# Decode attention with a KV cache: the last batch's K tile goes back behind the V tile of four batches earlier in the load queue

## The chip, the cores and the metric

The kernel runs on one core of a Trainium2 chip. The metric is the device time of one execution in microseconds (us); the kernel before took 373.58 us, the median of 8 runs from 372.36 to 374.9 us.

## What is computed

Thirty-two batches, four query positions each, 32 query heads sharing four K/V heads, 2048 cached positions, head size 128, all in bf16. One batch's K cache and its V cache are 2 MB each.

```python
q = (x @ wq).reshape(B, Sq, Hq, Dh).transpose(0, 2, 1, 3)
k = jnp.repeat(k_cache, rep, axis=1)
v = jnp.repeat(v_cache, rep, axis=1)
scores = jnp.einsum("bhqd,bhkd->bhqk", q, k) * (Dh ** -0.5)
p = softmax(scores, axis=-1)
o = jnp.einsum("bhqk,bhkd->bhqd", p, v)
out = o.transpose(0, 2, 1, 3).reshape(B, Sq, Hq * Dh) @ wo
# B, Sq, D = 32, 4, 1024; Hq, Hkv, Sk, Dh = 32, 4, 2048, 128
```

## The kernel before

The kernel writes an operation list for each engine in program order; every operation names those it must wait for, and the helper class `_Program` turns names into semaphore waits. Each engine works through its own list in order. So does SP, the engine that issues nearly all the transfers[...].

**Loads.** The buffer `big` has eight slots of 2 MB. The query weights `wq` take slots 0 to 3 at the start. After that the list `loads` (lines 159 to 164) gives the order of the 64 K and V tiles: K of batches 0 to 2, then alternately the K tile three batches ahead (`LEAD`) and the V tile of the current batch. Two further lines, 163 and 164, take K of the last batch, 31, out and put it directly behind K of batch 30. The tail of the list is therefore K30, K31, V27, V28, V29, V30, V31, where K31 means the K tile of batch 31. Tile number n goes to slot (4 + n) mod 8 (line 168). Its issue waits until the tile that held the slot is used up: for a K tile, its last transpose, `("kt", b, 3)`; for a V tile, the last matmul of its product with the probabilities, `("pv", b)`. K31 has place 58, slot 6, and waits for `pv` of batch 23; V27 has place 59, slot 7, and waits for `kt` of batch 27.

**Output weights.** Behind the 64 tiles SP issues `wo` in ten chunks (line 185), of 4, 4, 4, 4, 4, 4, 4, 2, 1 and 1 heads. Eight heads fill one slot, and the slots follow on: chunks 0 and 1 go where V26 was, chunks 2 and 3 where K30 was, chunks 4 and 5 to slot 6, chunks 6 to 9 to slot 7. Each chunk waits for the tile that last held its slot. So chunks 4 and 5 wait for the transposes of K31, chunks 6 to 9 for `pv` of V27.

**One batch i.** The steps, each a function in the kernel:
- `qd(i)`: GpSimd puts the queries of the batch in block-diagonal form (line 262).
- `kt(i)`: VectorE transposes the K tile in four pieces (line 271).
- `pe_qk(i)`: TensorE computes the scores into `ps_s`, 16 matmuls (lines 283 and 16). It waits for all four pieces and for exp of the batch before, which frees `ps_s`.
- `softmax_max(i)` on VectorE (lines 291 and 292), `softmax_exp(i)` on ScalarE (line 296).
- `pt(i)`: VectorE transposes the probabilities (line 304).
- `pd(i)`: GpSimd (for the last batch mostly VectorE) spreads them into `PD_sb` (line 316), once `pv` of the batch before has read it.
- `pe_pv(i)`: TensorE multiplies them by the V tile in 64 matmuls (line 323).
- `o_evac`, `pe_ot`, `ot_evac`: scaling, transposing and storing the result for the projection (lines 330, 336, 340).

**Order in the loop.** The engines overlap batches. Iteration i puts, in this order: `qd(i+1)` on GpSimd; pieces 0 and 1 of `kt(i+1)` on VectorE; the scores of i on TensorE; the maximum on VectorE; exp on ScalarE; pieces 2 and 3 of `kt(i+1)` and `pt(i)` on VectorE; then `pe_pv(i-2)` on TensorE and `pd(i-1)` on GpSimd. Thus on TensorE the product with V of batch 27 stands in iteration 29, directly ahead of the scores of batch 30; and on VectorE the first two pieces of K31 stand in iteration 30, directly ahead of the maximum of batch 30.

**The end.** After the last iteration come `pe_pv` of batches 30 and 31, and then the output projection `oproj` (lines 351 and 16): two matmuls a head, all 32 heads, chunk by chunk. It needs the finished output of the last batch and chunk c of `wo`. The result is copied out of `ps_s` in two halves (lines 359 and 360) and stored.

Of the kernel before, what the change touches and what calls it, by code (L numbers as in the profile page):

```python
# [78 lines left out]
def bass_standalone__gqa_block_cached__sampling_kernel(  # L79
# [8 lines left out]
    B, Sq, D = x.shape  # L88
# [21 lines left out]
    with ExitStack() as es:  # L110
# [48 lines left out]
        loads = [("k", b) for b in range(LEAD)]  # L159
        for b in range(B):  # L160
            loads += [("k", b + LEAD)] if b + LEAD < B else []
            loads += [("v", b)]
        loads.remove(("k", B - 1))
        loads.insert(loads.index(("k", B - 2)) + 1, ("k", B - 1))
        slot_of = {}
        holder = {s: "w" for s in range(NW)}
        for n, (kind, b) in enumerate(loads):
# [292 lines left out]
```

## Time and profile before

| | |
|---|---|
| median of 8 runs | 373.58 us (372.36 to 374.9) |
| profiled execution, its own time | 373.94 us |
| its span, first to last instruction | 372.2 us |
| TensorE matmuls busy | 279.5 us (75%) |
| VectorE busy | 275.3 us (74%) |
| GpSimd busy | 164.6 us (44%) |
| ScalarE busy | 123.0 us (33%) |
| bytes moved | 151.90 MB, mean 408 GB/s |
| mean granted TensorE clock | 0.953 |

The span begins with the first instruction of the profiled execution and ends with its last; the rest of the execution's time, 1.74 us, lies around it. All moments in the text below are us from the start of the span. Busy shares are means over the whole span; the steps near its end are read from the timeline, which gives for each instruction its start, its length, its engine and line, and in brackets the idle time of the engine before it with what ended it.

### The profile page before, as it was taken

What the parts mean: (1) busy time and instruction counts of PE and PEld (TensorE: products, weight loads), DVE (VectorE), ACT (ScalarE), POOL (GpSimd) and SP (SyncE); (2) the same over time, 40 slices, a digit from 0 to 9 for tenths busy, and PEclk for the clock granted to TensorE, in tenths of its full rate; (3) what the DMA queues carried; (4) which work ended last, traced back from release to release, by engine and by line L of the source; (5) the groups of instructions that cost most, each with busy time, mean ns of one, the idle gap of its engine ahead of it and who ended that gap; (6) DMA issues with size and microseconds to landing.
All of it is one profiled execution on the core that took longest, in us unless ns stands there. A gap on an engine that the chain in (4) does not pass through costs nothing.

```text
span 372.2 us, 5961 instructions
## 1 busy us (share of the span) xinstructions
PE 279.5 (75%) x2744; PEld 144.3 (39%) x2272; DVE 275.3 (74%) x273; ACT 123.0 (33%) x135; POOL 164.6 (44%) x262
## 2 busy tenths in 40 slices
PE   1972557888777778888888787887777876589796
PEld 1001003444444444444444545444333533545622
DVE  0029677999999999999999878799888699554300
ACT  1010211444444443333333333433433144247200
POOL 5001050555555555555554363655555555067100
PEclk9997888999999999999999898999998999699989
DMA  8999999999999999999999999999999999999960
GB/s 329 428 430 437 426 424 424 431 430 425 422 428 431 424 424 428 425 428 430 424 426 430 427 424 429 421 431 430 424 426 424 430 430 424 428 428 386 387 242 28
DMA packets 14507, 151.90 MB, mean 408 GB/s; under 512 B 1297, under 2 KB 1553, under 8 KB 5777
## 3 DMA queue, kind: packets, MB, share of 16 engines
q1 hardware_dynamic: 14336, 151.39, 96.7%
q8 instruction: 20, 0.33, 0.4%
q10 hardware_dynamic: 144, 0.13, 0.1%
q14 instruction: 7, 0.05, 0.0%
HBM read 151.26 MB, written 0.26 MB: 407 GB/s over the span
## 4 chain that ended last, share of the span: by engine, by line
DMA 33%; PE 32%; DVE 19%; ACT 8%; issue 7%; SPq 1%
DMA big<-in_v_cache_dram 27%; PE ps_s L16 18%; DVE mx L291 13%; ACT P_sb L296 7%; PE ps_s L283 6%; DMA big<-in_wq_dram 6%; PE ps_r L323 5%; DVE KT_sb L271 3%; PE ps_s L351 2%; DVE negmx L292 1%; DVE PD_sb L316 1%; DVE QT_sb L244 1%; DVE KT_sb L228 1%; SPq L156 0%; ACT QT_sb L340 0%
## 5 line engine op out<-in xcount | busy, mean ns | idle before, releaser
L316 POOL COPY PD_sb<-PT_sb 32x1024 f32<-32x1024 f32 x121 | 125.8, 1040 | 138.6 <-DVE KT_sb L271 62.4
L271 DVE STREAM_TRANSPOSE KT_sb<-big 128x1024 f32<-128x1024 f32 x128 | 150.7, 1217 | 5.2 <-DMA big<-in_k_cache_dram 5.1
L323 PE MATMUL ps_r<-big,PD_sb 128*128 128x128 bf16 x1984 | 121.7, 224 | 32.6 <-DMA big<-in_v_cache_dram 29.8
L323 PEld LDWEIGHTS ps_r<-big,PD_sb 128*128 128x128 bf16 x1984 | 117.4, 101 | 40.0 <-POOL QD_sb L262 23.2
L296 ACT ACTIVATE P_sb<-ps_s,negmx 128x2048 bf16<-128x2048 f32 x32 | 81.6, 2550 | 81.8 <-DVE negmx L292 81.8
L16 PE MATMUL ps_s<-KT_sb,QD_sb 128*128 128x512 bf16 x384 | 107.4, 388 | 0.0
L291 DVE TENSOR_REDUCE mx<-ps_s 128x1 f32<-128x2048 f32 x32 | 73.3, 2292 | 25.8 <-PE ps_s L16 25.4
L283 PE MATMUL ps_s<-KT_sb,QD_sb 128*128 128x512 bf16 x128 | 49.8, 389 | 43.0 <-ACT P_sb L296 36.8
L283 PEld LDWEIGHTS ps_s<-KT_sb,QD_sb 128*128 128x128 bf16 x128 | 12.6, 99 | 121.1 <-issue 73.1
L340 ACT ACTIVATE QT_sb<-ps_r 128x128 bf16<-128x128 bf16 x32 | 23.5, 735 | 104.5 <-PE ps_r L336 104.5
L304 DVE STREAM_TRANSPOSE PT_sb<-P_sb 128x1024 f32<-128x1024 f32 x32 | 39.9, 1246 | 14.6 <-ACT P_sb L296 14.6
L262 POOL COPY QD_sb<-QT_sb 32x64 f32<-32x64 f32 x128 | 29.6, 231 | 41.7 <-DVE QT_sb L244 26.1
L330 ACT ACTIVATE o_sb<-ps_r,rinv 128x128 bf16<-128x128 f32 x32 | 11.9, 373 | 19.7 <-PE ps_r L323 19.7
L228 DVE CAST KT_sb<-ps_r 128x512 bf16<-128x512 f32 x2 | 1.3, 686 | 20.7 <-PE ps_r L212 20.7
L359 DVE CAST y_sb<-ps_s 128x512 bf16<-128x512 f32 x1 | 0.7, 692 | 21.4 <-PE ps_s L351 21.4
L351 PE MATMUL ps_s<-big,QT_sb 128*128 128x512 bf16 x32 | 13.2, 412 | 0.9 <-ACT QT_sb L340 0.9
L16 PE MATMUL ps_s<-big,QT_sb 128*128 128x512 bf16 x32 | 13.1, 411 | 0.0
L336 PEld LDWEIGHTS ps_r<-ident,o_sb 128*128 128x128 bf16 x32 | 3.1, 96 | 23.8 <-issue 21.6
L351 PEld LDWEIGHTS ps_s<-big,QT_sb 128*128 128x128 bf16 x32 | 4.7, 147 | 11.4 <-issue 11.2
L16 PE MATMUL ps_s<-big,P_sb 128*128 128x512 bf16 x32 | 9.1, 410 | 0.0
L230 ACT ACTIVATE KT_sb<-ps_r 128x512 bf16<-128x512 f32 x2 | 1.1, 595 | 24.2 <-PE ps_r L16 24.2
L212 PEld LDWEIGHTS ps_r<-big,P_sb 128*128 128x128 bf16 x8 | 0.8, 104 | 20.4 <-issue 12.3
(30 smaller groups left out, 68.4 us busy)
## 6 DMA issues: line engine op xcount, KB each, us to landing
big<-in_k_cache_dram SPq DMA_DIRECT2D x32, 2048.0 KB, 28.7
big<-in_v_cache_dram SPq DMA_DIRECT2D x32, 2048.0 KB, 31.8
big<-in_wq_dram SPq DMA_DIRECT2D x4, 2048.0 KB, 14.6
big<-in_wo_dram SPq DMA_DIRECT2D x7, 1024.0 KB, 19.6
big<-in_wo_dram SPq DMA_DIRECT2D x1, 512.0 KB, 12.6
big<-in_wo_dram SPq DMA_DIRECT2D x2, 256.0 KB, 10.2
P_sb<-in_x_dram SPq DMA_DIRECT2D x1, 256.0 KB, 2.6
out_dram<-y_sb SPq DMA_DIRECT2D x1, 128.0 KB, 1.8
```

What stands on the lines that cost most here:

```text
L16: return eng.add_instruction(mybir.InstMatmult(name=nc.get_next_instruction_name(), engine=eng.engine, start_tensor_calc=start, stop_tenso ...
L262: p.op("pool", lambda e, s=src, d=dst: e.tensor_copy(d, s), waits if g == 0 else [], ("qd", i) if g == G - 1 else None)
L271: p.op("dve", lambda e, s=src, d=dst: e.transpose(d, s), waits, ("kt", i, c))
L283: mm = lambda e, a_=(out_, lhsT, rhs), f=first, l=last: e.matmul(a_[0], lhsT=a_[1], rhs=a_[2], start=f, stop=l, skip_group_check=True)
L291: p.op("dve", lambda e: e.tensor_reduce(mx[:, i % 4:i % 4 + 1], ps_s[:, :], AX.X, ALU.max), [("qk", i)], ("mx", i))
L296: p.op("act", lambda e: e.activation(P_sb[:, :, :, :].rearrange("p t r w -> p t w r"), ps_s[:, :].rearrange("p (t w r) -> p t w r", w=2, r=R),
L304: p.op("dve", lambda e: e.transpose(dst, src), [("exp", i)] + ([("pd", i - 2, G - 1)] if i > 1 else []), ("pt", i))
L316: p.op("dve" if i == B - 1 and g < 3 else "pool", lambda e, s=src, d=dst: e.tensor_copy(d, s), waits, ("pd", i, g))
L323: p.op("pe", lambda e, t=t: e.matmul(buf[:, 0:Dh], lhsT=pd_of(i)[:, t // 2, :, :, t % 2].rearrange("p g q -> p (g q)"), rhs=big[:, slot_of ...
L330: p.op("act", lambda e: e.activation(o_sb[:, :], buf[:, 0:Dh], ACT.Copy, scale=rinv[:, i % 4:i % 4 + 1]), [("pv", i), ("rinv", i)] + ([("o ...
L340: p.op("act", lambda e: e.activation(oT_sb[:, i * Sq:(i + 1) * Sq, :].rearrange("p s h -> p h s"), buf[:, 0:128].rearrange("p (h s) -> p h ...
L351: mm = lambda e, a=(out_, lhsT, rhs), h=h: e.matmul(a[0], lhsT=a[1], rhs=a[2], start=(h == 0), stop=(h == Hq - 1), skip_group_check=True)
```

## The change

Two lines are deleted, and nothing else. K31 stays where the loop puts it: the tail of the list becomes K30, V27, K31, V28, V29, V30, V31. V27 now has place 58 and slot 6, K31 place 59 and slot 7. The waits of the two places and of all later tiles are as they were, since they come from the tiles that held the slots before. With the two contents exchanged, `wo` chunks 4 and 5 wait for `pv` of V27, and chunks 6 to 9 for the transposes of K31. In the changed kernel every line after line 162 has a number lower by two.

```diff
         for b in range(B):
             loads += [("k", b + LEAD)] if b + LEAD < B else []
             loads += [("v", b)]
-        loads.remove(("k", B - 1))
-        loads.insert(loads.index(("k", B - 2)) + 1, ("k", B - 1))
         slot_of = {}
         holder = {s: "w" for s in range(NW)}
```

## The prediction

> **What bounds the kernel now.** First the page's chain of work that ended last, to see which resources lie on the path:
>
> ```profile
> ## 4 chain that ended last, share of the span: by engine, by line
> DMA 33%; PE 32%; DVE 19%; ACT 8%; issue 7%; SPq 1%
> ```
>
> DMA leads, so I looked where the chain runs through a load for the last time. The chain in order of time over the tail (start, length, what) shows it:
>
> ```profile
> 288.59 31.86 DMA big<-in_v_cache_dram
> 320.45 0.14 issue
> 320.58 5.14 PE ps_r L323 x64
> ...
> 329.22 2.30 DVE mx L291
> ...
> 334.50 0.38 PE ps_s L283
> ...
> 347.49 3.75 PE ps_r L323 x64
> ...
> 353.35 0.41 PE ps_s L351
> ```
>
> By program order the load is V of batch 27 (V27; K31 likewise), and from its landing at 320.45 everything to the end is compute: pv(27), the scores of 30 (325.56), their maximum, the scores of 31, pv(31), the output projection. No load ends a wait after it. The timeline gives the idle time ahead of each (in brackets, with what ended it):
>
> ```profile
> 276.56 3.73 PE L323 MATMUL ps_r<-big,PD_sb 128*128 128x128 bf16 x64 [2.54 <-DMA big<-in_v_cache_dram]
> ...
> 320.58 5.14 PE L323 MATMUL ps_r<-big,PD_sb 128*128 128x128 bf16 x64 [7.42 <-DMA big<-in_v_cache_dram]
> ...
> 329.22 2.29 DVE L291 TENSOR_REDUCE mx<-ps_s 128x1 f32<-128x2048 f32 x1 [7.42 <-PE ps_s L16]
> ```
>
> TensorE waits 2.54 us for an ordinary V and 7.42 us for V27, about one more tile; VectorE then idles 7.42 us behind it. K31, loaded ahead of V27, was waited for by nobody. Landings are issue time plus time to landing, asked for each load by itself (K31, V27, V28, then the wo chunk of heads 24 to 27):
>
> ```profile
> L173 SPq DMA_DIRECT2D big<-in_k_cache_dram x1: 328/328/328, 280.3 to 280.3; - x1
> DMA to landing us min/median/max: 35.2/35.2/35.2
> ...
> L173 SPq DMA_DIRECT2D big<-in_v_cache_dram x1: 327/327/327, 288.6 to 288.6; - x1
> DMA to landing us min/median/max: 31.9/31.9/31.9
> ...
> L173 SPq DMA_DIRECT2D big<-in_v_cache_dram x1: 328/328/328, 291.6 to 291.6; - x1
> DMA to landing us min/median/max: 35.1/35.1/35.1
> ...
> L185 SPq DMA_DIRECT2D big<-in_wo_dram x1: 2572/2572/2572, 346.4 to 346.4; - x1
> DMA to landing us min/median/max: 14.0/14.0/14.0
> ```
>
> So K31 landed at 280.3 + 35.2 = 315.5, V27 at 320.45, V28 at 326.7. The same question gave V29 331.4, V30 336.3, V31 341.8, and the ten wo chunks 344.5, 347.1, 349.8, 352.5, 355.3, 357.9, 360.4, 361.6, 362.3, 362.9. The queue never runs dry: 426 GB/s from 316 to 335 us, 387 from 335 to 354.
>
> [...] V27 was issued at 288.59, when the transposes of K27 end (288.57). [...] four landings from 305.8 (V26) to 320.45 lie 4.8 to 5.0 us apart. [...] Here the granted clock is 0.50 from about 316.7 to 323.5 and 354.3 to 357.7, which is why pv(27) took 5.14 and not 3.75 us. [...]
>
> **The change, part by part.**
> *The swap of two places.* No instruction is added or removed. The SP places 58 and 59 keep their slots and their waits (pv(23) and kt(27)), so they issue at 280.3 and 288.6 as before; only the contents change. Nothing earlier differs, so I give V27 the landing 315.5 and K31 320.45. I have no reason for other landings, since each moves 2 MB.
>
> *V27 earlier.* pv(27) starts at 315.63 instead of 320.58 (0.13 us from landing to start, as now): idle 2.5 instead of 7.4 us. It lasts 3.75 us warm, or about 5.2 if the clock drops on the 2.5 us pause, as it did at 286.33 (5.19). The scores of 30 then start at 319.2 or 320.8, ending 3.65 us later (325.56 to 329.22 now): 322.85 or 324.4.
>
> *K31 later.* Its first two transposes stand ahead of mx(30) on VectorE. They would run at 319.45 as now, but now wait to 320.5, and end 2.4 us later at 322.95. Thus mx(30) starts at 322.97 or 324.5, against 329.22. The new VectorE wait of about 1.1 us costs nothing, being covered by the scores of 30; what queues behind it is mx(30), kt(31)'s second half and P's transpose, and ScalarE's exp waits for mx. From mx to the end of exp takes 5.1 us (329.22 to 334.31): 328.1 or 329.6.
>
> *What is late next.* TensorE runs pv(28) before the scores of 31. V28 lands at 326.7, and GpSimd's copies for it finish 4.4 us after pv(27), at 323.8 or 325.4. So V28 decides in both cases: pv(28) at 326.83, and the scores of 31 follow 3.57 us later (266.77 to 270.34 in the steady stretch) at 330.4; exp(30) is done by then. Now they start at 334.50: gain 4.1 us. Of the 4.95 us by which V27 moves, plus the clock loss, 4.1 come through.
>
> *To the projection.* From the scores of 31 to the first projection matmul the chain takes 353.35 - 334.50 = 18.85 us. Later loads stay covered: pv(29) can start at 335.0 (V29 331.4), pv(30) at 339.4 (V30 336.3), pv(31) at 343.4 (V31 341.8). So the projection starts at 349.25.
>
> *The wo chunks.* Chunks 4 and 5 now wait for pv(27) (about 320) instead of kt(31) (333.98); chunks 6 to 9 for kt(31) (about 329) instead of pv(27). SP is still inside chunk 2's issue from 317.93 to 335.07, and only then reaches chunk 4. Both waits are over by then in either kernel, so I cost the exchange at nothing. Bound: if the 17 us were chunk 4's wait, the queue still held V30 and V31, so freeing it gains nothing either; it could lose 5.4 us if those packets overtook the V tiles (below). I keep zero.
>
> *The end.* 32 heads at 0.43 us (two matmuls 0.215 us apart) from 349.25 end at 363.0. But heads 24 to 27 need the chunk that lands at 360.4: 360.4 + 8 x 0.43 = 363.85. Adding 0.2 us for the last matmul's length, 364.05. A halved clock for one 3.4 us window, as now at 354.3, costs 1.7 us on the compute chain: 363.0 + 1.7 + 0.2 = 364.9. Now it is 369.05. The gain is 5.0 or 4.15 us; I take 4.6. Evacuation and store after it stay 3.15 us.
>
> The profiled execution took 373.94 us, 1.74 over its span. It would become 369.3. The median of the runs is 0.36 us lower: 373.58 - 4.6 = 369.0.
>
> **Rivals.**
> *Landings drift (a smaller gain).* V28 landed 6.2 us after V27, not 4.9, and the last chunks land one by one with DMA share falling from 1.05 to 0.04 between 357 and 363[...]. If V28 or the wo chunks slip by 2 to 3 us, they bind and the gain is 2: about 371.5. Against: the bytes and their order outside the two places are unchanged.
> *K31 takes V27's place as the stall (no change).* Were K31 to land at 326.7, one further place back, exp(30) would end at 326.7 + 2.5 + 5.1 = 334.3, as now: 373.6. Against: its place is the one whose load landed at 320.45, with about 2.3 us of cover beyond that.
> *wo overtakes V (slower).* [...] At 387 GB/s they are 5.4 us; put wholly ahead of V28 it lands at 332.1, the scores of 31 start at 335.8 instead of 334.5, and the time is 374.9. The sign turns where V28 slips by over 4.1 us. For it: V28's extra 1.3 us comes after chunks 0 and 1 were issued. Against: K31 and V27, also after chunk 0's issue, landed on schedule, and SP stands in chunk 2.
> *The change doing nothing* is excluded if landings follow the queue: the stall is on the chain, and 7.4 us is far above the ordinary 2.5.
>
> **How the numbers follow.** Forecast 0.80 (about 368.6 to 369.5, or 367.7 if the chunks also land earlier and no clock window is lost, 363.2 against 369.05); small gain 0.11 (to 371.5); no change 0.04; overtaking 0.05. A difference under 0.3% (1.1 us) can't be told from no change here. The first two are faster: 0.91. The range goes from 367.2 to 371.3: it covers both clock cases, earlier chunks with half a us for the spread of the runs, and most of the small gain.
>
> **What would show it.** After: pv(27) starts near 315.6 with about 2.5 us idle; VectorE waits about 1 us on K31; mx(30) starts at 323 to 324.5; pv(28) waits for V28; the scores of 31 start near 330.4, the projection near 349; some projection matmul waits for a wo chunk or the clock drops there. It would be wrong if V27 lands late all the same, if V28 to V31 land over 2 us later than listed, or if SP's last wo issues move.

## The result and the profile after

The changed kernel takes 369.36 us, the median of 11 runs (368.42 to 371.73), against 373.41 us for the kernel before, the median of 32 runs. The medians differ by 4.05 us. The ratio, which is taken over all the runs and not from the medians, is 0.9909 with a 95% interval from 0.989 to 0.9927; that is 3.4 us, since the four longest of the changed kernel's runs weigh in it. The forecast was 369.0 in a range from 367.2 to 371.3. The profiled execution is not a typical one. It took 371.73 us (span 369.9) and belongs to a group of four runs between 370.9 and 371.7; the other seven lie between 368.4 and 369.5. What follows of the trace must be read with that in mind.

The page's chain of the changed kernel comes first. The share of loads has grown from 33% to 42%. Most of that comes from earlier in the span: this execution's chain runs through four V loads where the other ran through three. The last load adds 5 us (36.81 instead of 31.86):

```profile
## 4 chain that ended last, share of the span: by engine, by line
DMA 42%; PE 29%; DVE 15%; ACT 7%; issue 5%; SPq 1%; POOL 0%; POOLq 0%
```

The same chain in order of time (start, length, what). All lines have numbers two lower than before:

```profile
289.37 36.81 DMA big<-in_v_cache_dram
326.31 6.11 PE ps_r L321 x64
...
335.93 2.30 DVE mx L289
...
345.27 3.75 PE ps_r L321 x64
...
351.13 0.42 PE ps_s L349
```

The load is now V28, landing at 326.2, and pv(28) takes V27's former part. Before, the chain left the loads at 320.45, but with pv(27) and one more batch still to come; the projection began at 353.35, now at 351.13. The timeline shows each step between:

```profile
314.97 3.73 PE L321 MATMUL ps_r<-big,PD_sb 128*128 128x128 bf16 x64 [2.53 <-DMA big<-in_v_cache_dram]
...
321.30 2.37 DVE L269 STREAM_TRANSPOSE KT_sb<-big 128x1024 f32<-128x1024 f32 x2 [2.42 <-DMA big<-in_k_cache_dram]
...
323.60 2.25 DVE L289 TENSOR_REDUCE mx<-ps_s 128x1 f32<-128x2048 f32 x1
...
326.31 6.11 PE L321 MATMUL ps_r<-big,PD_sb 128*128 128x128 bf16 x64 [4.09 <-DMA big<-in_v_cache_dram]
...
332.26 0.38 PE L281 MATMUL ps_s<-KT_sb,QD_sb 128*128 128x512 bf16 x1
```

pv(27) waits 2.53 us, as for any V tile, instead of 7.42. VectorE waits 2.42 us for K31. pv(28) waits 4.09 us for V28 and then takes 6.11 instead of 3.75 us. The busy times by stretch say why (behind the stretch stand its length and TensorE's busy time; TensorE's granted clock is the third entry from the end):

```profile
321.09:324.50 3.41, 1.14 (x6) 0.10 (x1) 3.20 (x3) 0.74 (x1) 2.92 (x6) 1.00 0.96 408
324.50:327.91 3.41, 1.59 (x16) 1.62 (x17) 3.38 (x4) 1.84 (x1) 0.00 (x0) 0.50 1.06 452
327.91:331.33 3.42, 3.42 (x35) 3.42 (x33) 1.70 (x3) 3.42 (x3) 0.00 (x0) 0.50 0.97 412
```

The granted clock was 0.50 from 324.5 to 331.3, that is for 6.8 us. The wait set this off: experiment 4 fills the wait, and there the clock is 1.00 from 322 to 332. It was 0.50 again for 3.4 us, 351.8 to 355.2, at the start of the projection, as before the change (354.3 to 357.7).

### The profile page after: what moved, and what is told of

It is laid out like the page before. It is cut to its first block, busy times and chain, and to the rows that moved or that the text cites. A ratio compares the mean times of both kernels' runs of the same rounds, so it can differ in the third digit from the quotient of the medians.

```text
span 369.9 us, 5961 instructions
## 1 busy us (share of the span) xinstructions
PE 280.7 (76%) x2744; PEld 144.0 (39%) x2272; DVE 275.3 (74%) x273; ACT 123.1 (33%) x135; POOL 164.6 (44%) x262
## 4 chain that ended last, share of the span: by engine, by line
DMA 42%; PE 29%; DVE 15%; ACT 7%; issue 5%; SPq 1%; POOL 0%; POOLq 0%
DMA big<-in_v_cache_dram 37%; PE ps_s L16 15%; DVE mx L289 10%; PE ps_r L321 6%; ACT P_sb L294 6%; DMA big<-in_wq_dram 6%; PE ps_s L281 5%; DVE KT_sb L269 3%; PE ps_s L349 2%; DVE PD_sb L314 1%; DVE QT_sb L242 1%; DVE KT_sb L226 1%; DVE negmx L290 1%; SPq L156 0%; POOL PD_sb L314 0%
```

## The experiments

A ratio is to the kernel before, run beside the experiment on the same chip, and is again taken over all the runs. The changed kernel's 369.36 us were measured apart from these.

**1. The exchange of the wo chunks by itself.**

```diff
-        wo_slot = [(NW + n + c) % NS for c in range(NW)]
+        wo_slot = [(NW + n + c) % NS for c in (0, 1, 3, 2)]
```

> The kernel before, with its own load order; only the wo chunks are exchanged between the last two slots, so that chunks 4 and 5 wait for pv(27) and chunks 6 to 9 for the transposes of K31, as in the changed kernel. Theory (the place of V27 and K31 in the queue is the whole change): no difference, 373.4 us, since SP stands in chunk 2's issue until 335. Rival (chunk 4's wait for K31 until 334 held up SP and the wo stream): this alone gives the gain, 369.4.

Measured: 373.56 us, ratio 1.0005 (0.9987 to 1.0022). No difference. The issue of chunk 2 (duration in ns, start in us), first in the changed kernel, then here:

```profile
L183 SPq DMA_DIRECT2D big<-in_wo_dram x1: 17555/17555/17555, 317.2 to 317.2; - x1
```

```profile
L185 SPq DMA_DIRECT2D big<-in_wo_dram x1: 14465/14465/14465, 320.2 to 320.2; - x1
```

It ends at 317.2 + 17.6 = 334.8 and 320.2 + 14.5 = 334.7; before the change it was 317.9 + 17.1 = 335.1. It ends at the same moment whatever the chunks behind it wait for. So the 17 us are not the wait of chunk 4 for K31, and the order of those waits costs nothing. What holds SP up for these 17 us was not shown.

**2. Before, with V27's wait taken away.** Batch 27's product reads the tile of V26, so this kernel's output for that batch is another; K31 stays early.

```diff
-                    rhs=big[:, slot_of["v", i], t, :], ...
+                    rhs=big[:, slot_of["v", i - (i == 27)], t, :], ...
-                    waits + ... + [("v", i)] ...
+                    waits + ... + [("v", i - (i == 27))] ...
```

(The wo chunks in these two slots also wait for pv(27) and for V27's landing.)

> The kernel before, with K31 still ahead of V27, but batch 27's product reads the tile of V26, so nothing waits for V27 (which is still loaded). Theory (the 7.4 us wait for V27 is the loss, and K31's later place costs nothing): as the changed kernel, 369.4, with pv(28) waiting for V28 at about 326.5. Rival (in the changed kernel K31's lateness costs something, hidden behind the gain): clearly below 369.4, by up to the 1.3 us that VectorE lost there. Rival (TensorE's clock alone): the clock still falls in the idle time, and it stays near 373.

Measured: 371.17 us, ratio 0.9932 (0.9907 to 0.9957). Faster than before, so the wait was on the path, but 1.8 us above the 369.4 expected, though the intervals of the two ratios overlap. Its runs are of the same two kinds: two near 369, eight from 370.7 to 372.0. In the profiled one (371.07) pv(28) again waits for V28, and again takes longer than at full clock (5.36 instead of 3.75 us):

```profile
326.30 5.36 PE L323 MATMUL ps_r<-big,PD_sb 128*128 128x128 bf16 x64 [3.28 <-DMA big<-in_v_cache_dram]
```

It starts at the changed kernel's moment, 326.3, although K31 stands as early in the list as before the change. That supports that K31's lateness costs nothing in the end. The size of the expectation was missed, and why most of these runs are of the slower kind is open.

**3. K31 one place further back.**

```diff
+        loads.remove(("k", B - 1))
+        loads.insert(loads.index(("v", B - 4)) + 1, ("k", B - 1))
```

> The changed kernel with K31 one place further back, behind V28. Theory (VectorE's wait for K31 has about 2.3 us of cover and no more): K31 lands near 326.3, the maximum of batch 30 starts near 328.8 instead of 323.6, exp ends near 333.8, and the scores of 31 start near 334, as before the change; 373.1, or up to 375 if TensorE's clock falls in its idle time of 7 us. Rival (V tiles alone matter, and the earlier V28 is a gain): 367 to 369.

Measured: 375.06 us, ratio 1.0037 (1.002 to 1.0053): slower than before the change. VectorE's line for K31, and TensorE's first scores of 31:

```profile
326.26 2.37 DVE L271 STREAM_TRANSPOSE KT_sb<-big 128x1024 f32<-128x1024 f32 x2 [7.38 <-DMA big<-in_k_cache_dram]
...
333.75 0.38 PE L283 MATMUL ps_s<-KT_sb,QD_sb 128*128 128x512 bf16 x1 [2.92 <-ACT P_sb L296]
```

Now K31 is what comes last: VectorE waits 7.38 us, and the scores of 31 start at 333.75 (334 expected). Another 1.7 us come from slower matmuls after TensorE's wait for exp: from the start of the first score matmul to the end of the last (339.06) it takes 5.3 instead of 3.65 us. Those at 335.91 and 337.62 last 0.63 us each, the one at 333.75 lasts 0.38; in the projection of the changed kernel the same two lengths go with a granted clock of 0.50 and of 1.00. So moving K31 further back is not always a gain. One place too far for K31 costs at least as much as one place too far for V27.

**4. TensorE kept busy while it waits for V28.** The added matmuls write the bank that pv(28) overwrites.

```diff
+        def warm(buf, waits, n):
+            for _ in range(n):
+                p.op("pe", lambda e: e.matmul(buf[:, 0:128], lhsT=ident[:, :], rhs=ident[:, :],
+                                              start=True, stop=True, skip_group_check=True), waits)
         def pe_pv(i):
             buf, waits = slot(("o", i))
+            if i == B - 4:
+                warm(buf, waits, 56)
```

> The changed kernel with 56 matmuls of the identity by itself ahead of pv(28), into the bank that pv(28) then overwrites; they fit in the 4.1 us for which TensorE waits for V28. Theory (that idle time halves the clock for pv(28), which then takes 6.1 instead of 3.75 us on the path): pv(28) back at 3.75, the scores of 31 start near 330 instead of 332.3, and the time falls by 1 to 2.4 us, to 367.0 to 368.4, where the last wo chunks begin to bind. Rival (the clock loss is absorbed by the wo chunks anyway): 369.4.

Measured: 368.83 us in six runs, ratio 0.9891 (0.9852 to 0.9931). The interval is too wide to set it apart from the changed kernel; its profiled run, 368.31 us, span 366.5, shows the mechanism:

```profile
322.43 3.29 PE L319 MATMUL ps_r<-ident 128*128 128x128 bf16 x56
...
326.24 3.73 PE L328 MATMUL ps_r<-big,PD_sb 128*128 128x128 bf16 x64 [0.52 <-DMA big<-in_v_cache_dram]
...
359.74 0.44 PE L356 MATMUL ps_s<-big,QT_sb 128*128 128x512 bf16 x1 [0.48 <-DMA big<-in_wo_dram]
```

pv(28) starts as in the changed kernel but takes 3.73 us, at a granted clock of 1.00. The projection, about 2.4 us earlier, then waits 0.48 us for the wo chunk of heads 24 to 27, which lands at 359.7. That is the next bound, where the prediction had put it.

**5. The same, and the pauses ahead of the projection.** Ahead of the last batch's transpose and behind it:

```diff
             buf, waits = slot(("ot", i))
+            if i == B - 1:
+                warm(buf, waits, 14)
...
         pe_ot(L)
+        warm(*slot(None), 14)
```

> The kernel of the fourth experiment with 14 more matmuls of the identity in each of the two pauses ahead of the output projection. Theory (with the clock kept up, the path ends at the landing of wo chunk 6, near 359.7, plus 8 heads): 368.2, no lower than the best runs of the fourth experiment, and with less spread. Rival (the clock loss ahead of the projection was also on the path): up to 1.7 us lower than the fourth experiment.

Measured: 368.37 us in four runs (368.19 to 369.77), ratio 0.9866 (0.9836 to 0.9896). As the theory said, it is no lower than the best of experiment 4; the interval still overlaps the changed kernel's. The profiled run, the slowest (369.77 us), shows what is left:

```profile
316.53 5.36 PE L328 MATMUL ps_r<-big,PD_sb 128*128 128x128 bf16 x64 [3.96 <-DMA big<-in_v_cache_dram]
...
325.25 3.29 PE L319 MATMUL ps_r<-ident 128*128 128x128 bf16 x56
...
328.38 3.74 PE L328 MATMUL ps_r<-big,PD_sb 128*128 128x128 bf16 x64
```

V27 landed only at 316.4, TensorE idled 3.96 us ahead of pv(27), and that product took 5.36 us (granted clock 0.62 from 318 to 322). The added matmuls, queued behind it, then did harm: V28 had landed at 326.1, and GpSimd's copies for pv(28) can be put at 326.3 (an estimate: the end of pv(27), 321.9, and the 4.4 us of the prediction), but pv(28) started at 328.38, 2 us late. So such matmuls cost time where the wait that they should fill is shorter than they are, as here.

**6. After, with V28's wait taken away.** As experiment 2, for batch 28, which reads the tile of V27; that batch's output is another.

```diff
-                    rhs=big[:, slot_of["v", i], t, :], ...
+                    rhs=big[:, slot_of["v", i - (i == 28)], t, :], ...
-                    waits + ... + [("v", i)] ...
+                    waits + ... + [("v", i - (i == 28))] ...
```

> The changed kernel, but batch 28's product reads the tile of V27, so that nothing waits for V28 (which is still loaded). Theory (V28 is the load that decides in the changed kernel): pv(28) starts near 323.5, the scores of 31 start when exp ends, near 328.5 instead of 332.3, the projection 3 to 4 us earlier, and the wo chunks bind: 368.2. Rival (K31 and VectorE decide): as the changed kernel, 369.4.

Measured: 368.40 us in four runs (368.16 to 369.25), ratio 0.9872 (0.9845 to 0.9899). The time is as expected, though with four runs the interval still overlaps the changed kernel's. The profiled run shows less than hoped: there pv(27) lost the clock (6.19 us after a pause of 3.86 us; granted 0.60 from 314 to 318 and 0.55 from 318 to 322) and GpSimd's copies came last:

```profile
327.13 3.75 PE L321 MATMUL ps_r<-big,PD_sb 128*128 128x128 bf16 x64 [0.98 <-POOL PD_sb L314]
```

At 327.13 V28 had landed anyhow (326.1), so this run doesn't show the expected start at 323.5. The best runs stop at 368.2 like those of 4 and 5, which fits a common bound behind them.

**7 and 9. Before, with TensorE kept busy while it waits for V27.** First ahead of pv(27) alone:

```diff
             buf, waits = slot(("o", i))
+            if i == B - 5:
+                warm(buf, waits, 112)
```

> The kernel before with 112 matmuls of the identity by itself ahead of pv(27), 6.2 us, inside its 7.4 us wait for V27. Theory (the wait itself is the loss, and the halved clock in pv(27) only its 1.4 us extra): pv(27) 3.75 us, 372.0. Rival (the clock was most of the loss): near 369.4.

Measured: 373.54 us, ratio 1.0004 (0.9987 to 1.002). A miss, and the trace says why:

```profile
313.15 6.41 PE L321 MATMUL ps_r<-ident 128*128 128x128 bf16 x112
...
321.55 5.36 PE L330 MATMUL ps_r<-big,PD_sb 128*128 128x128 bf16 x64 [1.98 <-DMA big<-in_v_cache_dram]
```

1.98 us of idle time remained, and the clock fell all the same (0.59 from 322 to 326). So it was repeated with 144 matmuls, and with experiment 5's two sets of 14 ahead of the projection:

```diff
-                warm(buf, waits, 112)
+                warm(buf, waits, 144)
```

> The kernel before with 144 matmuls of the identity ahead of pv(27), so that nearly all of its wait is filled (with 112 about 2 us of idle time were left and pv(27) still took 5.36 us), and 14 in each of the two pauses ahead of the projection, as in the fifth experiment. Theory (the late V27 is the larger part, the clock the smaller): pv(27) 3.75 us but still not before 320.5 to 321.5; 371.3 to 371.8, so 3 us above the fifth experiment. Rival (with the clock kept up the two orders are alike): 368.4.

Measured: 371.75 us in 22 runs (371.44 to 372.45), ratio 0.9963 (0.9952 to 0.9974).

```profile
314.03 8.20 PE L321 MATMUL ps_r<-ident 128*128 128x128 bf16 x144
...
322.07 3.74 PE L330 MATMUL ps_r<-big,PD_sb 128*128 128x128 bf16 x64
```

pv(27) is back at 3.74 us, and the old order still needs 371.75 - 368.37 = 3.4 us more than the new one in experiment 5. The two ran on different chips; the difference of their ratios, 0.0097, says 3.6 us. A part of it is the added matmuls themselves: in experiment 7's profile, with the same order, V27 landed at 321.4 and pv(27) started at 321.55; here they held it back until 322.07, some 0.5 us by this estimate. So about 3 us are the order. Keeping the clock up (0.958 to 0.968 in the mean of a run, against 0.949 to 0.959) saved the old kernel 373.15 - 371.75 = 1.4 us (373.15 is the kernel before on that chip); an estimate without that delay is 2 us.

**8. The next bound pushed back.** Experiment 5 with wo chunk 6 cut in two:

```diff
-    WO = (4, 4, 4, 4, 4, 4, 4, 2, 1, 1)
+    WO = (4, 4, 4, 4, 4, 4, 2, 2, 2, 1, 1)
```

> The fifth experiment with wo chunk 6 (four heads) split in two of two heads. Theory (the landing of chunk 6 sets the end): the bound falls from 359.7 + 8 heads to about 361 + 4 heads or the chain of compute, so 367.7 to 368.0. Rival (something else ends the path): as the fifth experiment.

Measured: 367.85 us in four runs (367.69 to 368.01), ratio 0.9853 (0.9828 to 0.9879). The fastest of all, and below the changed kernel's interval. Projection and pv(28) in its profile:

```profile
326.17 3.73 PE L328 MATMUL ps_r<-big,PD_sb 128*128 128x128 bf16 x64 [0.80 <-DMA big<-in_v_cache_dram]
...
348.62 0.41 PE L358 MATMUL ps_s<-big,QT_sb 128*128 128x512 bf16 x1
```

From 348.62 on the projection has one gap of 0.2 us left (near 360.8) instead of the 0.48 us of experiment 4. The median is 0.5 us below that of experiment 5.

## Why the prediction was right, step by step

*V27 a place earlier.* Right: landing 314.8 (315.5 forecast), pause 2.53 us (2.5), pv(27) 3.73 us (3.75 or 5.2). Experiment 2 shows that this wait was on the path, and 9 against 5 that the order itself is worth about 3 us with the clock taken out. But the landing is not the same in every execution: in the profile of experiment 8 pv(27) started at 314.99 after a pause of 1.76 us, in those of 5 and 6 V27 came at 316.4 and 316.3. In these two TensorE idled 3.96 and 3.86 us, and pv(27) took 5.36 and 6.19 us. What moves the landing was not found.

*K31 a place later, at no cost.* Right in the end, but the scores of 30, named first, did not cover the wait. VectorE's wait was 2.42 us, not 1.1: V27's place was served earlier (314.8) and K31 later (321.3) than assumed. The scores of 30 were done at about 322.2, so the maximum of batch 30, at 323.60, waited 1.4 us for K31 and not for the scores. That was absorbed one step on: exp(30) ended at 328.6, and the scores of 31 stand behind pv(28), which even at full clock would have let them start only at 326.31 + 3.57 = 329.9 (in experiment 4, at full clock, pv(28) took 3.73 us in all). The cover is therefore V28, with 1.3 us to spare instead of the 2.3 forecast; experiment 3 uses it up and turns the gain into a loss.

*V28 decides next.* Right in place and time: pv(28) at 326.31 (326.83). The mis-sized term is the length of pv(28). I gave it 3.57 us to the scores of 31, having looked for the halved clock at pv(27) and at the projection, not at the longer pause of 4.09 us that the change itself makes here. In the profiled run it was 332.26 - 326.31 = 5.95 us, 2.4 more, and the scores of 31 started at 332.26, not 330.4; in experiment 4, with the pause filled, the 2.4 us are gone. From there to the projection it took 18.87 us (18.85 forecast).

*The wo chunks.* The exchange costs nothing, as forecast (experiment 1). The landing of the chunk of heads 24 to 27 was put at 360.4 and came at 359.7. In the profiled run of the changed kernel it did not bind, since the clock had made the projection late; in experiment 4 it did, and 8 moved it.

*The sum.* 4.6 us were forecast and 4.05 measured. The profiled execution, which lost clock ahead of the scores of 31 and in the projection, took 371.73; experiment 4's, with a mean granted clock of 0.967 against 0.952, took 368.31. That the two groups of the changed kernel's runs differ by the clock is likely (0.948 to 0.953 mean clock in the upper four, 0.957 and more in five of the seven below). But only one run of them has a trace, and the landing of V27 may differ too. The forecast took the mean of a case with and a case without one halved stretch of 3.4 us in the projection, and knew nothing of the larger loss at pv(28). That its sum came within 0.6 us of the median is therefore partly luck. Which wait ends last at each step was forecast rightly.

*The rivals.* Packets of wo did not overtake V28: chunk 4, which with chunk 5 makes 2.1 MB, was issued at 335.36, hardly sooner than before (335.67), and V28 landed at 326.2. The landings did not drift: V29 to V31 came at 331.0, 336.0 and 340.8, up to 1 us earlier than listed. K31 in V27's part of the stall is what experiment 3 built, with the load landing at 326.3, where the rival had 326.7: there the whole gain is gone, as it says, and the slower matmuls take more (375.06 instead of the 373.6 worked out).

## What to carry to other kernels

Where loads are one queue that never runs dry (here 428 GB/s from 316 to 335 us and 388 from 335 to 354 after the change), moving a tile forward moves another back by about the same time (here V27 5.7 us forward and K31 5.8 us back); ask of both which operation stands first behind them on its engine, and what that operation still waits for otherwise. Place a tile for the consumer with the least cover, here V27 ahead of the scores, and check the tile behind the one pushed back, too. And where a wait on TensorE is made longer, count the slower clock that may follow as part of the wait (2.4 us at pv(28) in the profiled run).

## What was not expected of the hardware

The prediction left open whether a pause of about 2.5 us is followed by a halved clock. A pause of 1.98 us on TensorE after 6.4 us of uninterrupted work was (experiment 7, 0.59 from 322 to 326), while one of 2.53 us passed without it in the changed kernel. A pause of 4.09 us was followed by 6.8 us at 0.50, the second half of them wholly while the product was running (3.42 of 3.42 us busy). So the length of a pause alone does not tell.

The profiles of the two kernels show more. In each of them the changes of the granted clock from 60 us up to the end of the matmuls lie whole multiples of 3.41 us apart (in the changed kernel's at 61.68, 246.00, 249.41, 266.48, 269.89, 324.50, 331.33, 351.81 and 355.22). Cut at that step, the two hold 168 stretches of 3.41 us at full clock. After each of the seven in which TensorE's matmuls were busy for less than 43% the clock was halved, after none of the 157 with more than 47%, and after two of the four in between. These are counts of two profiles. The pause of 2.53 us left a stretch that was busy for 1.59 us (46.6%), and the next kept its clock:

```profile
310.85:314.26 3.41, 1.59 (x9) 0.19 (x2) 3.32 (x3) 0.73 (x1) 3.08 (x6) 1.00 0.95 404
314.26:317.67 3.41, 2.70 (x49) 2.73 (x50) 2.97 (x5) 2.62 (x2) 0.23 (x1) 1.00 1.04 442
```

In the kernel before, a pause of the same length, 2.52 us ahead of the product at 286.33, left 1.22 us (36%), and the clock was halved:

```profile
282.60:286.01 3.41, 1.22 (x7) 0.11 (x2) 3.32 (x2) 0.73 (x1) 3.00 (x6) 1.00 1.00 428
286.01:289.42 3.41, 3.09 (x30) 3.12 (x31) 3.00 (x5) 2.59 (x2) 0.00 (x0) 0.50 0.98 418
```

The pause of 4.09 us left 1.14 us (33%; the first line of the stretches shown with the result). So in these profiles it counts, beside its length, where between two such moments a pause falls. The moments don't lie alike in both: one was at 316.73 in the kernel before and at 317.67 in the changed one. This fits that executions of one kernel differ in the clock that they lose, but the run times alone don't show it. What holds a clock that is already halved was not worked out. At 0.50 the projection's matmuls start 0.43 us apart instead of 0.215, so a halved stretch of 3.41 us costs at most 1.7 us, an estimate from these two numbers.
